# A fused retention and feed-forward kernel: another order of loads, products and vector work in its first block

## The chip, the core and the metric

The kernel runs on one core of a Trainium2 chip. The metric is the device time of one execution in microseconds, where less is better. Besides the times of whole executions there is one profiled execution, whose trace gives the start and the length of every instruction on the engines: PE (TensorE, with PEld for its weight loads), DVE (VectorE), ACT (ScalarE), POOL (GpSimd) and SP (SyncE, which here only issues DMAs).

## The reference

Per batch and head a state is carried along the sequence, and the result goes through a feed-forward layer. Inputs are float32, with 4 batches, 8 heads, 768 positions and a head dimension of 64; the layer has 512 inputs and 2048 hidden units.

```python
gamma = 1.0 - 2.0 ** (-5.0 - np.arange(H))
for t in range(S):
    state = gamma * state + np.einsum('bhd,bhe->bhde', k[:, :, t], v[:, :, t])
    y[:, :, t] = D ** -0.5 * np.einsum('bhd,bhde->bhe', q[:, :, t], state)
x = y.transpose(0, 2, 1, 3).reshape(B * S, H * D)      # 3072 x 512
h = x @ w_in                                           # 512 x 2048
g = h * np.tanh(np.log1p(np.exp(h)))                   # Mish
out = g @ w_out                                        # 2048 x 512
```

## The kernel before

The 3072 tokens are 24 chunks of 128 tokens. A chunk's attention is done in matrix form: the scores of its keys against its queries (`scores`), a triangular mask with the decay folded into q and v (`mask`, on DVE), the product of the masked scores with v (`present`), the product of q with the state of the chunks before (`past`), and the update of the state by an outer product of k and v (`outer`). Present and past add up in one bank of PSUM, and a copy on ACT turns the sum into `xt`, the input of the layer. The layer is done by blocks of chunks: the first block has four chunks (512 tokens, `CPB` = 4), and the ten blocks that follow have two each. All inputs are cast to float16 on the way, with sums in float32.

The layer's matrix products save multiplications by the scheme of seven products in place of eight (Strassen's, in Winograd's form). For that, sums of quarters of each operand are made on DVE: `wsums` from w_in, `tmats` from w_out (`weight_sums`, four for each half), `gsums` from g, and `tsums` from x. In the first block the first product (`g1`) is done plainly, with 16 steps of 128 hidden units each followed by a Mish on ACT. Its second product (`first_g2`) takes the seven products for the slices 0 and 2 of w_out, each slice having 512 hidden units, and plain products for the slices 1 and 3; the plain products of slice 3 (`end`) close each output. Each product in `first_g2` is done for two pairs of chunks, and the results meet in four banks: `px`, `pz`, `pb` and `pe`.

The order of instructions on each engine is the order in which the code emits them, because the schedule is manual: every engine has its own queue and works through it in order, and semaphores make it wait for its operands and for buffers. Work that another engine's progress should delay is put in at a named point: `plan` in `first_block` lists what is emitted after which step of the first product, and `late` is a list of small DVE jobs that `some_late(n)` takes from the front. `gate(x)` is a tiny copy on POOL that makes all POOL work behind it wait until x is written.

Buffers come from pools that rotate. The staging pool `rn_wstage` has four buffers of 8 KB per partition under the tag `wt`: they hold in turn the first block's q, the four slices of w_in, output slices, and then the float16 sums. Another pool, with the tag `g`, has two buffers that hold the other two output slices and later g. PSUM has four banks for products (`mm`) and two double banks for attention (`at`), each reused in rotation: a tile waits until the one before it in the same place has been read.

In the first block the queries come in two halves by heads (`load_first_q`, line 200), and k and v come for two pairs of chunks (s = 0 and 1) and two halves of heads each (`load_two`). `turn_first_q` and `turn_two` transpose on PE, `first_q_out` and `turned_two` copy the result out of PSUM, `cast_two` casts k on ACT and v on POOL. `spin` and `spin_wide` are matmuls whose results are not used. From line 802 on, `first_block` writes out the order: casts and turns, `scores_half` and `mask_half` for the four combinations of s and half, `outer_first` and `state_first` for the states, `present_first` and `past_first` for the output of attention, `xt_out`, and then the first product, of which the first two steps are split into halves of tokens (`first_g1`). `load_weights` (line 778) issues the loads of the weights on SP's queue, and behind them q and v of the chunks 4 and 5 (`load_one`); `load_more` issues the last output slice in two halves and q and v of the next chunks. k of the later chunks is brought by POOL's own DMA queue (`bring_k`). `first_g2` also holds the attention of the chunks 4 and 5, which the second block takes as its input (`y_two(1, False)` near its end).

Of the kernel before, what the change touches and what calls it, by code (L numbers as in the profile page):

```python
# [16 lines left out]
def kernel(  # L17
# [135 lines left out]
    def load_w(which, s):  # L153
        if which == "in":
            t = wstage.tile([P, NBP, TB], FP32, name="wi", tag="wt", bufs=4)
            n = TB // 2 if s < 2 else TB
            for o in range(0, TB, n):
                nc.sync.dma_start(t[:, :, o:o + n], win_ap[:, :, s * TB + o:s * TB + o + n])
        else:
            if s < NSL // 2:  # L160
                t = wstage.tile([P, FPS, d_model], FP32, name="wt", tag="wt", bufs=4)
            else:
                t = gp.tile([P, FPS, d_model], FP32, name="wt", tag="g")
            if s < NSL - 1:
                nc.sync.dma_start(t, wout_ap[:, s * FPS:(s + 1) * FPS])  # L165
        wtmps[which, s] = t
# [31 lines left out]

    def load_first_q():

        qf = wstage.tile([P, H, CPB, D], FP32, name="qfirst", tag="wt", bufs=4)
        for a in range(0, H, H // 2):
            nc.sync.dma_start(
                qf[:, a:a + H // 2],
                q[0, a:a + H // 2, :TB].rearrange("h (p r) d -> p h r d", r=CPB))
        return qf

    def turn_first_q(qf, half):
        a, n = half * (H // 2), H // 2
        q16 = castp.tile([P, CPB, n, D], FP16, name="qfirst16", bufs=1, tag=f"qfirst16_{half}")  # L210
        nc.vector.tensor_tensor(
            q16.rearrange("p r h d -> p h r d"), qf[:, a:a + n],
            qs_spread[:, a:a + n].unsqueeze(3).broadcast_to((P, n, CPB, D)), op=ALU.mult)
# [6 lines left out]
    def first_q_out(half, t_ps, eng):  # L220
        n = HP // 2
        dst = qfirst_t[:, half * n:(half + 1) * n].rearrange("p i (t r) -> p i t r", r=CPB)
        src = t_ps.rearrange("p i r t -> p i t r")
        if eng is nc.scalar:
            nc.scalar.copy(dst, src)
        else:
            eng.tensor_copy(dst, src)

# [29 lines left out]

    def turned_two(s, half):
        n = HP // 2  # L260
        nc.scalar.copy(kts[s][:, half * n:(half + 1) * n], t16s.pop((s, half)))

# [58 lines left out]

    def xt_out(g, y, eng, n=1):
        if eng is nc.scalar:
            nc.scalar.copy(xts[0][:, g:g + n], y[:, g % 2:g % 2 + n])
        else:
            eng.tensor_copy(xts[0][:, g:g + n], y[:, g % 2:g % 2 + n])

# [450 lines left out]
    def load_weights():  # L778
        for s in range(NSL):
            load_w("in", s)  # L780
        for s in range(NSL):
            load_w("out", s)
        room(CPB)
        room(CPB + 1)
        for g in (CPB, CPB + 1):
            load_one(g, 0, nc.sync)
            load_one(g, 2, nc.sync)

    def load_more():
        load_last_wout(0)  # L790
        load_last_wout(1)
        nload[0] += 2
        load_to(CPB + 4)
# [7 lines left out]

    def first_block():
        qf = load_first_q()
        for s in range(2):
            for nm in "kv":
                for half in range(2):
                    load_two(nm, s, half)
        nload[0] = CPB
# [6 lines left out]
        spin(at, 8)  # L815
        tq = turn_first_q(qf, 0)
        spin_wide(at, 3)
        first_q_out(0, tq, nc.scalar)
        tq = [tq, turn_first_q(qf, 1)]
# [21 lines left out]
        state_first(0)  # L841
        at = at_tile()
        scores_half(1, 0, at)
        mask_half(1, 0, at)
        y = atps.tile([P, 2, HP, C], FP32, name="y_ps", tag="at")
        present_first(0, y, range(HP))
        turn_two(1, 1)
        turned_two(1, 1)
        state_first(1)
        past_first(1, y)  # L850
        xt_out(0, y, nc.scalar, 2)
        for half in range(2):
            cast_two("v", 1, half)
        cast_win(0, 0, nc.gpsimd)
        at = at_tile()
        scores_half(1, 1, at)
        mask_half(1, 1, at)
        y = atps.tile([P, 2, HP, C], FP32, name="y_ps", tag="at")
        outer_first(1)
        state_first(2)  # L860
        present_first(1, y, range(HP // 2))
        h_ps = [mmps.tile([P, 1, TB], FP32, name="h_ps", tag="mm") for _ in range(2)]
        first_g1(h_ps[0], 0, 0)
        present_first(1, y, range(HP // 2, HP))
        past_first(2, y)
        past_first(3, y)
        xt_out(2, y, nc.scalar)
        xt_out(3, y, nc.vector)
        first_g1(h_ps[1], 1, 0)
# [5 lines left out]
        for s in range(1, NSL):  # L875
            for half in range(2):
                cast_win(s, half, nc.vector)
            if s == 2:
                late.extend(win_sums())
            if s >= 2:  # L880
                some_late(4)
        room_for_sums()
        plan = {9: [(cast_wout, 0), (room_for_more,), (bring_first,)],
                10: [(some_late, 1)], 13: [(cast_wout, 1), (room_for_more,)], 16: [(load_more,)]}
        late.extend(weight_sums(0) + weight_sums(1))
        for u in range(2, NFB):
            g1(0, u)
            for fn, *args in plan.get(u + 1, ()):
                fn(*args)
        first_g2()  # L890
        hsnaps.append(gp.tile([P, 4, TB], FP32, name="hsnap", tag="g0"))

    def bring_first():
        gate(wtmps["out", 1][:, 0, :1])
        bring_k(CPB)
        bring_k(CPB + 1)

    def first_g2():
        hf = d_model // 2
        sub = ALU.subtract  # L900
        pairs = range(CPB // 2)
# [25 lines left out]

        def g_part(s, i):
            g = gtiles[0, s // 2][:, s % 2 * FPS:(s % 2 + 1) * FPS]
            return g.rearrange("p f (a i t) -> p f a i t", a=2, i=2)[:, :, :, i]  # L930

        def g_sum(dst, x, y, f):
            d = sums[:, dst - 1].rearrange("p f (a t) -> p f a t", a=2)
            nc.vector.tensor_tensor(d, x, y, op=f)

        def the_sum(i):
            return sums[:, i - 1].rearrange("p f (a t) -> p f a t", a=2)
# [4 lines left out]
        g_sum(1, g_part(0, 1), g_part(2, 1), ALU.add)  # L942
        g_sum(2, the_sum(1), g_part(0, 0), sub)
# [8 lines left out]
        some_late(1)  # L952
        g_sum(3, g_part(0, 0), g_part(0, 1), sub)
        g_sum(4, g_part(2, 0), the_sum(2), sub)
        some_late(1)
        for p in pairs:
            mm(pz[p], a(p, 1, 1), b(1, 1))
        for p in pairs:
            mm(pb[p], a(p, 0, 1), b(1, 0))
        for p in pairs:  # L960
            mm(pb[p], a(p, 0, 2), b(2, 0))
        for p in pairs:
            mm(pe[p], a(p, 0, 1), b(1, 1))
        for p in pairs:
            mm(px[p], sm(p, 2), t(2))
            nc.scalar.copy(osb[p][0][:, 1], px[p])
        turn(CPB, True)
        for p in pairs:
            mm(px[p], sm(p, 3), t(3))
            nc.vector.tensor_tensor(osb[p][1][:, 1], px[p], m5[p], op=ALU.add)  # L970
        bring_k(CPB + 2)
        cast_v(CPB + 1)
        bring_k(CPB + 3)
        for p in pairs:
            mm(pe[p], sm(p, 4), b(2, 1))
        some_late(1)
        scores(CPB)
        turn(CPB + 1)
        mask(CPB)
        cast_wout(3, FPS)  # L980
        for p in pairs:
            mm(px[p], a(p, 1, 2), t(4))
# [18 lines left out]

        end(0, 0)
        end(0, 1)
        y_two(1, False)
# [102 lines left out]
```

## Time and profile before

| | |
|---|---|
| Time, median of 3 executions | 200.63 us (200.55 to 201.08) |
| The profiled execution | 200.17 us |
| Its span, from the first to the last instruction | 198.4 us |
| PE busy in the span | 190.2 us (96%) |
| DVE busy | 144.8 us (73%) |
| ACT busy | 114.9 us (58%) |
| POOL busy | 82.5 us (42%) |
| Granted TensorE clock | 1.0 all along |
| Moved by DMA | 36.05 MB, 182 GB/s on average |

A line of the order in time gives the start and the length of a group of like instructions in microseconds, the engine, the line of the kernel, the operation, what it writes and reads, the shape, and how many there are; in brackets stands how long the engine was idle before it and what ended that. A line of the busy times by stretch gives the stretch, its length, the busy time and number of instructions of each engine in it, the granted clock, the share of time in which the DMA engines were busy, and what they moved in GB/s. A busy engine is the bound of a stretch only where nothing makes it wait; where PE has gaps, what ended them has to be looked for.

### The profile page before, as it was taken

What the parts mean: (1) busy time and instruction counts of PE and PEld (TensorE: products, weight loads), DVE (VectorE), ACT (ScalarE), POOL (GpSimd) and SP (SyncE); (2) the same over time, 40 slices, a digit from 0 to 9 for tenths busy, and PEclk for the clock granted to TensorE, in tenths of its full rate; (3) what the DMA queues carried; (4) which work ended last, traced back from release to release, by engine and by line L of the source; (5) the groups of instructions that cost most, each with busy time, mean ns of one, the idle gap of its engine ahead of it and who ended that gap; (6) DMA issues with size and microseconds to landing.
All of it is one profiled execution on the core that took longest, in us unless ns stands there. A gap on an engine that the chain in (4) does not pass through costs nothing.

```text
span 198.4 us, 5725 instructions
## 1 busy us (share of the span) xinstructions
PE 190.2 (96%) x2363; PEld 157.7 (79%) x2363; DVE 144.8 (73%) x294; ACT 114.9 (58%) x220; POOL 82.5 (42%) x110
## 2 busy tenths in 40 slices
PE   6897999999999999999999999999999999999992
PEld 2355546974987988988988988988988988988982
DVE  3786698998898597597498597597498596596362
ACT  2463667243673675675664774774754765765840
POOL 7072005695646708708606707707615614110000
PEclk9999999999999999999999999999999999999999
DMA  5999999999999999997997996997996967201102
GB/s 170 302 311 354 384 388 318 196 298 176 166 259 225 180 188 226 202 145 156 188 162 156 157 168 146 179 176 93 244 195 84 202 90 61 102 3 53 56 26 79
DMA packets 95897, 36.05 MB, mean 182 GB/s; under 512 B 82304, under 2 KB 89984, under 8 KB 95872
## 3 DMA queue, kind: packets, MB, share of 16 engines
q1 hardware_dynamic: 74928, 33.04, 76.3%
q0 software_dynamic: 20800, 2.62, 21.0%
q8 instruction: 18, 0.29, 0.7%
q14 instruction: 7, 0.06, 0.1%
q10 hardware_dynamic: 144, 0.03, 0.1%
HBM read 27.30 MB, written 6.29 MB: 169 GB/s over the span
## 4 chain that ended last, share of the span: by engine, by line
PE 78%; SPq 7%; DMA 6%; DVE 4%; ACT 2%; issue 1%; DVEq 0%
PE o_ps L727 30%; PE h_ps L654 18%; PE h_ps L630 16%; SPq L140 5%; DMA wt<-in_moe_w_out_dram 4%; PE y_ps L463 3%; PE at L397 3%; DMA qfirst<-in_q_dram 2%; PE y_ps L454 2%; PE o_ps L924 2%; PE h_ps L798 1%; SPq L165 1%; PE u_ps L412 1%; DVE gsum L705 1%; SPq L170 1%
## 5 line engine op out<-in xcount | busy, mean ns | idle before, releaser
L654 PE MATMUL h_ps<-xt,win 128*128 128x256 f16 x320 | 41.5, 273 | 0.0
L647 DVE TENSOR_TENSOR hsum<-h_ps,hsnap 128x512 f32<-128x512 f32 x30 | 19.8, 688 | 20.9 <-PE h_ps L630 18.9
L727 PEld LDWEIGHTS <-gsum 128*128 128x128 f16 x320 | 30.8, 98 | 4.0 <-DVE gsum L705 0.4
L654 PEld LDWEIGHTS <-win 128*128 128x128 f16 x320 | 29.3, 98 | 3.6
L727 PE MATMUL o_ps<-tmat,gsum 128*128 128x256 f16 x240 | 27.8, 273 | 0.0
L727 PEld LDWEIGHTS <-g 128*128 128x128 f16 x240 | 23.3, 98 | 2.9
L641 ACT ACTIVATE g<-hsum 128x512 f16<-128x512 f32 x30 | 18.6, 630 | 11.4 <-DVE hsum L647 11.2
L403 DVE TENSOR_TENSOR am<-at,tri 128x1024 f16<-128x1024 f32 x20 | 24.3, 1215 | 0.0
L347 POOL TENSOR_TENSOR v<-vf,qvs 128x512 f16<-128x512 f32 x20 | 23.5, 1177 | 0.4 <-PE o_ps L924 0.4
L661 ACT ACTIVATE g<-h_ps 128x512 f16<-128x512 f32 x40 | 22.9, 603 | 0.8 <-PE h_ps L654 0.6
L637 ACT COPY hsnap<-h_ps 128x512 f32<-128x512 f32 x30 | 16.4, 582 | 11.2 <-PE h_ps L630 11.2
L336 POOL TENSOR_TENSOR qk<-qf,qvs 128x512 f16<-128x512 f32 x20 | 21.6, 1080 | 2.1 <-DMA qf<-in_q_dram 2.1
L355 POOL COPY gate<-gsum 128x1 f16<-128x1 f16 x9 | 1.6, 183 | 48.4 <-DVE gsum L701 48.4
L741 DVE TENSOR_TENSOR osb<-o_ps,snap 128x256 f32<-128x256 f32 x30 | 12.5, 418 | 12.4 <-PE o_ps L727 10.9
L733 ACT COPY snap<-o_ps 128x256 f32<-128x256 f32 x30 | 11.2, 372 | 16.0 <-PE o_ps L727 15.7
L630 PEld LDWEIGHTS <-wsum 128*128 128x128 f16 x320 | 19.5, 98 | 0.5
L727 PE MATMUL o_ps<-wout,g 128*128 128x256 f16 x160 | 19.3, 273 | 0.0
L342 POOL DMA_DIRECT2D qk<-in_k_dram x20 | 18.8, 942 | 0.0
L630 PE MATMUL h_ps<-xsum,wsum 128*128 128x128 f16 x240 | 16.7, 219 | 0.0
L500 ACT CAST xt<-y_ps 128x1024 f16<-128x1024 f32 x10 | 10.1, 1013 | 10.6 <-PE y_ps L454 10.6
L630 PEld LDWEIGHTS <-win 128*128 128x128 f16 x240 | 15.1, 98 | 0.7
L435 ACT COPY stx<-stc 64x256 f16<-64x256 f16 x30 | 12.0, 400 | 2.0 <-POOL stc L429 1.8
(119 smaller groups left out, 306.9 us busy)
## 6 DMA issues: line engine op xcount, KB each, us to landing
vf<-in_v_dram SPq DMA_DIRECT2D x24, 256.0 KB, 5.7
out_dram<-osb SPq DMA_DIRECT2D x22, 256.0 KB, 4.9
qf<-in_q_dram SPq DMA_DIRECT2D x20, 256.0 KB, 5.4
wt<-in_moe_w_out_dram SPq DMA_DIRECT2D x3, 1024.0 KB, 8.9
qk<-in_k_dram POOLq DMA_DIRECT2D x20, 128.0 KB, 5.5
wi<-in_moe_w_in_dram SPq DMA_DIRECT2D x4, 512.0 KB, 7.3
wi<-in_moe_w_in_dram SPq DMA_DIRECT2D x2, 1024.0 KB, 11.3
qfirst<-in_q_dram SPq DMA_DIRECT2D x2, 512.0 KB, 5.1
```

The source lines that it names most:

```text
L336: nc.gpsimd.tensor_tensor(room16(g)[0], loaded[g][0], qs.unsqueeze(2).broadcast_to((P, H, D)), op=ALU.mult)
L342: nc.gpsimd.dma_start(room16(g)[1], k[b, :, c * C:(c + 1) * C].rearrange("h p d -> p h d"))
L347: nc.gpsimd.tensor_tensor(room16(g)[2], loaded[g][2], vs.unsqueeze(2).broadcast_to((P, H, D)), op=ALU.mult)
L403: nc.vector.tensor_tensor(am, ats.pop(g), tri.unsqueeze(1).unsqueeze(1).broadcast_to((P, 2, HP, C)), op=ALU.mult)
L630: nc.tensor.matmul(h_ps[:, f], w(f, d), x(d), start=first and f == 0 and d == 0, stop=d == n - 1, skip_group_check=True)
L637: nc.scalar.copy(x, h_ps)
L641: nc.scalar.activation(gt[:, 2 * i * FPS:(2 * i + 1) * FPS, j * P:(j + 1) * P], h, AF.Mish, scale=inv_boost3)
L647: nc.vector.tensor_tensor(h, h_ps, x, op=ALU.add)
L654: nc.tensor.matmul(h_ps[:, j], win(s, 2 * half + j, bp), xt(blk, bp), start=bp == 0, stop=bp == NBP - 1)
L661: nc.scalar.activation(gt[:, fb:fb + 2], h_ps, AF.Mish, scale=inv_boost3)
L727: nc.tensor.matmul(o_ps, x(f), w(f), start=first and f == 0, stop=f == n - 1, skip_group_check=True)
L741: nc.vector.tensor_tensor(dst, o_ps, plus, op=ALU.add)
```

## The change

It reorders the first block; the computation is the same.

- Front: k's first half of heads is loaded before the second half of q. The cast of q is taken out of its transposition. The second half of q is cast half on DVE and half on POOL, after the turn of k's first part, and turned only after the first scores and mask. Copies change engines: the second half of q goes out on ACT instead of DVE, the turned k of s = 0 on DVE instead of ACT; `xt_out` is one ACT copy of two chunks each time. One of the unused products goes. `outer_first(0)` stands ahead of the turn of the next k; y of the first two chunks comes after the last scores and mask instead of before; the casts of the second v come earlier.
- Output slices: they are loaded in the order 0, 2, 1, 3; slices 0 and 2 lie in the staging pool, 1 and 3 in the other. The two halves of slice 3 are issued among q and v of the chunks 4 and 5 instead of after them. Slices 1 and 3 are cast half on DVE and half on ACT.
- First product: four of the eight sums of w_in are left for later (`wsum_late`). The sums of g are made during the first product (`g_sum`) instead of in `first_g2`, with the casts of slices 0 and 2 and the first four sums of w_out between them.
- Second product: the products of slices 0 and 2 come first, the plain ones of slice 1 after them. POOL's gate ahead of the casts of chunk 4 is on the last of the four sums of w_out instead of the second. At the end, one sum of w_out, the scores and the mask of chunk 5 and the outer product of chunk 4 come behind `end(0, 0)` instead of ahead of it, with the outer product behind the scores and the mask.

The core of the diff:

```diff
-            if s < NSL // 2:
+            if s % 2 == 0:
                 t = wstage.tile([P, FPS, d_model], FP32, name="wt", tag="wt", bufs=4)
...
+    def cast_first_q(half, engines):
...
+        m = n // len(engines)
+        for e, eng in enumerate(engines):
+            b = slice(a + e * m, a + e * m + m)
+            eng.tensor_tensor(
+                q16[:, :, e * m:e * m + m].rearrange("p r h d -> p h r d"), raw["q"][:, b],
+                qs_spread[:, b].unsqueeze(3).broadcast_to((P, m, CPB, D)), op=ALU.mult)
...
-    def turned_two(s, half):
+    def turned_two(s, half, on_act=False):
...
+        if on_act:
+            nc.scalar.copy(dst, src)
+        else:
+            nc.vector.tensor_copy(dst, src)
...
+    def xt_out(g, y):
+        nc.scalar.copy(xts[0][:, g:g + 2], y)
...
-        for s in range(NSL):
+        for s in (0, 2, 1, 3):
             load_w("out", s)
...
+        load_one(CPB, 0, nc.sync)
+        load_one(CPB, 2, nc.sync)
+        load_last_wout(0)
+        load_one(CPB + 1, 0, nc.sync)
+        load_last_wout(1)
+        load_one(CPB + 1, 2, nc.sync)
...
     def first_block():
...
+        load_first_q(0)
+        load_two("k", 0, 0)
+        load_first_q(H // 2)
+        load_two("k", 0, 1)
...
+        cast_first_q(0, [nc.vector])
+        tq = turn_first_q(0)
         cast_two("k", 0, 0)
         turn_two(0, 0)
-        first_q_out(1, tq[1], nc.vector)
+        first_q_out(0, tq)
         turned_two(0, 0)
-        cast_two("k", 0, 1)
         spin_wide(at, 3)
+        cast_first_q(1, [nc.vector, nc.gpsimd])
         scores_half(0, 0, at)
         mask_half(0, 0, at)
+        cast_two("k", 0, 1)
+        tq = turn_first_q(1)
+        first_q_out(1, tq)
...
         cast_two("k", 1, 0)
+        outer_first(0)
         turn_two(1, 0)
-        turned_two(1, 0)
+        turned_two(1, 0, True)
         cast_two("k", 1, 1)
-        outer_first(0)
         state_first(0)
+        for half in range(2):
+            cast_two("v", 1, half)
...
             if s == 2:
                 late.extend(win_sums())
-            if s >= 2:
                 some_late(4)
         room_for_sums()
-        plan = {9: [(cast_wout, 0), (room_for_more,), (bring_first,)],
-                10: [(some_late, 1)], 13: [(cast_wout, 1), (room_for_more,)], 16: [(load_more,)]}
         late.extend(weight_sums(0) + weight_sums(1))
+        wsum_late = [late.pop(0) for _ in range(4)]
+        plan = {9: [(g_sum, 3)],
+                12: [(g_sum, 1), (cast_wout, 0), (room_for_more,), (bring_first,), (g_sum, 2),
+                     (some_late, 1)],
+                14: [(cast_wout, 2), (room_for_more,), (some_late, 2), (g_sum, 4),
+                     (some_late, 1)],
+                16: [(load_more,)]}
...
         for p in pairs:
             mm(pe[p], sm(p, 1), t(1), True)
             nc.scalar.copy(m5[p], pe[p])
-        cast_wout(2)
-        some_late(1)
-        gate(tmats[0][:, 1, 0, :1])
+        for p in pairs:
+            mm(pb[p], a(p, 0, 2), b(2, 0))
+        for p in pairs:
+            mm(px[p], sm(p, 2), t(2))
+            nc.scalar.copy(osb[p][0][:, 1], px[p])
+        cast_wout(1, 2)
+        gate(tmats[1][:, 1, 0, :1])
         casts(CPB)
         cast_q(CPB + 1)
...
+        for p in pairs:
+            mm(px[p], sm(p, 3), t(3))
+            nc.vector.tensor_tensor(osb[p][1][:, 1], px[p], m5[p], op=ALU.add)
+        for p in pairs:
+            mm(pe[p], sm(p, 4), b(2, 1))
+        for fn in wsum_late:
+            fn()
+        for p in pairs:
+            mm(px[p], a(p, 1, 2), t(4))
         for p in pairs:
             mm(pb[p], a(p, 0, 1), b(1, 0))
         for p in pairs:
+            mm(pz[p], a(p, 1, 1), b(1, 1))
         turn(CPB, True)
         bring_k(CPB + 2)
         cast_v(CPB + 1)
         bring_k(CPB + 3)
         for p in pairs:
+            mm(pe[p], a(p, 0, 1), b(1, 1))
         scores(CPB)
+        cast_wout(3, 2)
+        mask(CPB)
         turn(CPB + 1)
         for p in pairs:
             mm(px[p], a(p, 1, 1), b(1, 0))
-        outer_wide(CPB)
         casts(CPB + 2)
         turn_and_load(CPB + 2)
         cast_q(CPB + 3)
-        scores_one(CPB + 1)
-        decay_wide(CPB)
...
         end(0, 0)
+        some_late(1)
+        scores_one(CPB + 1)
+        outer_wide(CPB)
+        decay_wide(CPB)
         end(0, 1)
         y_two(1, False)
```

More of the change, by code (lines that the diff above doesn't have):

```diff
@@ L218, in turn_first_q, with first_q_out @@
         return t_ps
-    def first_q_out(half, t_ps, eng):
+    def first_q_out(half, t_ps):
         n = HP // 2
[L222 to L227, printed above, removed]
+        nc.scalar.copy(
+            qfirst_t[:, half * n:(half + 1) * n].rearrange("p i (t r) -> p i t r", r=CPB),
+            t_ps.rearrange("p i r t -> p i t r"))
     def load_two(nm, s, half):
@@ L320, in past_first @@
                 start=False, stop=True, skip_group_check=True)
[L322 to L326, printed above, removed]
+    def xt_out(g, y):
+        nc.scalar.copy(xts[0][:, g:g + 2], y)
     def room16(g):
@@ L836, in first_block @@
         cast_two("k", 1, 0)
+        outer_first(0)
         turn_two(1, 0)
-        turned_two(1, 0)
+        turned_two(1, 0, True)
         cast_two("k", 1, 1)
-        outer_first(0)
         state_first(0)
+        for half in range(2):
+            cast_two("v", 1, half)
         at = at_tile()
@@ L844, in first_block @@
         mask_half(1, 0, at)
-        y = atps.tile([P, 2, HP, C], FP32, name="y_ps", tag="at")
-        present_first(0, y, range(HP))
+        state_first(1)
         turn_two(1, 1)
[L848 to L854, printed above, removed]
+        turned_two(1, 1, True)
         at = at_tile()
@@ L889, in first_block, with g_sum, part, first_g2 @@
                 fn(*args)
-        first_g2()
+        first_g2(wsum_late)
         hsnaps.append(gp.tile([P, 4, TB], FP32, name="hsnap", tag="g0"))
     def bring_first():
-        gate(wtmps["out", 1][:, 0, :1])
+        gate(wtmps["out", 2][:, 0, :1])
         bring_k(CPB)
         bring_k(CPB + 1)
-    def first_g2():
+    def g_sum(n):
+        def part(s, i):
+            g = gtiles[0, s // 2][:, s % 2 * FPS:(s % 2 + 1) * FPS]
+            return g.rearrange("p f (a i t) -> p f a i t", a=2, i=2)[:, :, :, i]
+        s1, s2, s3, s4 = [
+            gsums[0].rearrange("p s (f a) t -> p s f a t", a=2)[:, i] for i in range(4)]
+        dst, x, y, f = {
+            1: (s1, part(0, 1), part(2, 1), ALU.add), 2: (s2, s1, part(0, 0), ALU.subtract),
+            3: (s3, part(0, 0), part(0, 1), ALU.subtract),
+            4: (s4, part(2, 0), s2, ALU.subtract)}[n]
+        nc.vector.tensor_tensor(dst, x, y, op=f)
+    def first_g2(wsum_late):
         hf = d_model // 2
-        sub = ALU.subtract
         pairs = range(CPB // 2)
```

80 lines of the change are left out of this document (19 added, 61 removed).

## The prediction

> **What bounds the kernel now.** I read the page's first part for the bound, then busy time by stretch for where that bound breaks down, then the order of time in the first block, where all of the edits lie.
>
> ```profile
> PE 190.2 (96%) x2363; PEld 157.7 (79%) x2363; DVE 144.8 (73%) x294; ACT 114.9 (58%) x220; POOL 82.5 (42%) x110
> ```
>
> ```profile
> 0.00:20.70 20.70, 16.45 (x235) 9.41 (x236) 12.98 (x30) 8.86 (x14) 8.85 (x19) 1.00 1.00 288
> 20.70:32.80 12.10, 12.10 (x58) 5.49 (x57) 10.25 (x18) 8.40 (x15) 1.05 (x1) 1.00 1.05 383
> 32.80:49.78 16.98, 16.76 (x173) 12.58 (x172) 15.19 (x20) 7.12 (x12) 12.88 (x13) 1.00 1.43 223
> 49.78:195.00 145.22, 144.88 (x1901) 130.21 (x1899) 106.02 (x227) 90.50 (x180) 59.70 (x79) 1.00 0.94 147
> ```
>
> The columns after the length are the busy times of PE, PEld, DVE, ACT and POOL, the granted clock, the DMA share and GB/s. From 49.78 us, where the second block starts, PE is busy 144.88 of 145.22 us. Nothing can be regained there, so I take a shift of that start to reach the end one for one. Only the first block has to be worked out: the attention front (to 20.7), the first product (to 32.8), and the output product with the next chunks' attention (to 49.78, DVE busy 15.19 of 16.98).
>
> The front and the tail of the first block, in order of time:
>
> ```profile
> 9.68 2.08 POOL L245 TENSOR_TENSOR v<-vf,qvs 128x512 f16<-128x512 f32 x2 [5.17 <-DMA vf<-in_v_dram]
> ...
> 10.01 0.42 PE L274 MATMUL at<-qfirst_t,qkt 64*64 64x128 f16 x16
> ...
> 18.87 0.69 DVE L326 CAST xt<-y_ps 128x512 f16<-128x512 f32 x1 [1.50 <-ACT xt L324]
> 19.30 1.36 PE L798 MATMUL h_ps<-xt,win 128*128 128x256 f16 x11 [0.97 <-issue]
> ```
>
> ```profile
> 37.28 1.50 POOL L336 TENSOR_TENSOR qk<-qf,qvs 128x512 f16<-128x512 f32 x1
> ...
> 37.79 1.53 DVE L934 TENSOR_TENSOR gsum<-g,gsum 128x1024 f16<-128x1024 f16 x1
> ...
> 42.39 0.69 DVE L388 COPY qkt<-t_ps 128x1024 f16<-128x1024 f16 x1 [0.17 <-PE t_ps L383]
> ...
> 42.99 1.22 DVE L403 TENSOR_TENSOR am<-at,tri 128x1024 f16<-128x1024 f32 x1
> ...
> 44.20 1.04 ACT L186 CAST wout<-wt 128x1024 f16<-128x1024 f32 x1 [0.43 <-DMA wt<-in_moe_w_out_dram]
> ...
> 44.36 0.69 DVE L445 TENSOR_TENSOR su<-u_ps,st 128x512 f32<-128x512 f32 x1
> ...
> 44.96 1.21 DVE L403 TENSOR_TENSOR am<-at,tri 128x1024 f16<-128x1024 f32 x1
> 45.29 0.96 PEld L924 LDWEIGHTS <-g 128*128 128x128 f16 x5 [0.37 <-issue]
> 46.09 0.92 DVE L449 TENSOR_TENSOR st<-su,gcm 128x512 f16<-128x512 f32 x1
> 46.67 0.48 PEld L463 LDWEIGHTS <-v 128*64 128x64 f16 x16 [0.42 <-issue]
> ...
> 48.84 0.69 DVE L995 TENSOR_TENSOR osb<-o_ps,osb 128x512 f32<-128x512 f32 x1 [0.89 <-PE o_ps L924]
> ```
>
> The reader is to see two things. The last half of output slice 3 lands at 44.17, its ACT cast ends at 45.25, and PE loses 0.37 for it. And the Vector work between the next two chunks' scores and PE's use of the new state (mask, su, mask, st: 42.99 to 47.0) ends just as PE comes to the second "past" product at about 47.3, so it is hidden with nothing to spare.
>
> **The front.** The first k half (256 KB) goes ahead of the second q half. Eight pieces between q's landing at 6.83 and v's last give some 0.92 us each (v at 9.68 is the third, at 13.22 the seventh). So k lands at about 6.2 and the last half of q at 7.75 instead of 6.83; its cast, now half on DVE (0.62) and half on POOL (1.06 by L245), ends at 8.9, and POOL has nothing else until v at 9.68. The ACT cast of k (0.62) moves under DVE's q cast, DVE takes the 0.4 of the copy out (half of L388's 0.69), and the first scores start after ACT's q copy at 8.4, not 10.01. That 1.6 us does not carry. The bytes ahead of v are the same, so POOL's first two v casts still end at 11.8. The outer products now stand ahead of the next turn on PE's queue, so turn and scores of the second half follow them: turn 12.3, ACT copy to 13.3 (0.59), scores 13.3, mask 13.9 to 15.1 (now 13.81 to 15.02), state to 15.8 (0.69), last mask to 17.0, last state to 17.7. PE then does four products of y (0.42), the early h (0.55) and the past (0.45) to 18.4; one ACT copy of both chunks (1.02 by L324) replaces 0.59 on ACT followed by 0.69 on DVE, and ends at 19.6, where the old pair ended at 19.56. Eight matmuls later the first product runs on at 20.6 (now 20.71). Worth -0.1, with -0.5 to +0.4 as bounds, the lower if the masks leave DVE earlier, the upper from a repeat of part of the 0.97 "issue" gap. The warming product that goes (0.86) filled idle time. The second pair of v casts moves earlier in POOL's order but waits for its landing (13.22) as now.
>
> **The loads.** Slices are 1 MB each; the casts that waited show landings at 31.70 and 34.51, so 2.8 apart. In the order 0, 2, 1, 3 slice 2 takes slice 1's place and the other way round; slice 0 may be issued earlier, because its buffer is released by a DVE cast that no longer stands behind an xt copy, but the queue is full (383 GB/s) and I give nothing for it. On SP's queue the halves of slice 3 pass q and v of chunk 5. A 256 KB q or v takes some 1.3 there (estimate: two halves of slice 3 landed 1.5 apart, four such loads lie between slice 2 and the first half, 8.2 us with k's), so slice 3 is complete at about 42.6 and q of 5 lands at 41.1 instead of before 40.2, v of 5 near 44. Cast time of slice 3 stays 1.05 on ACT, now beside 0.69 on DVE. The wait of 0.37 goes; what is late next is Vector work.
>
> **The Vector line up to the seven products.** Four sums of w_in (4 x 0.42) leave 27.7 to 29.2 for later, one g sum (0.68) goes in, and then the second (with slice 2 of g) waits for the Mish of the twelfth product, about 30.05 (the sixteenth ends at 33.6, one per 0.865). So DVE idles some 1.6. From there: sum 0.68, slice 0 cast 1.22 (32.0), sum 0.69, weight sum 0.69 (33.4), slice 2 cast 1.22 (34.65), two weight sums (36.05), sum 0.69, weight sum 0.69 (37.45), half of slice 1 0.69, two additions 0.74 (38.9). The single-time 0.69 instead of 1.53 is right as POOL's gate now waits for the fourth weight sum. PE, at 0.87 per product (32.80 to 33.67): first 32.7, second 33.6, third would start at 34.45 and waits for slice 2, +0.25; the fourth and fifth use the same bank without a turn between them, so the fifth waits for ACT's copy (it starts 0.63 after the fourth starts, then 2 x 0.4), +0.2; the seventh waits for the additions, +0.2; then two plain products, the turn of chunk 4 at 41.2, one product, and scores, which need ACT's qkt copy: 1.7 after the turn starts (38.91 to 40.57 now, with two products between), so +0.35 at 42.9. POOL's casts of 4 and q of 5 end by 42.2, in time for the turn of 5 at 43.2. Total on this stretch +1.0, of which 0.13 was already there before the scores; bounds 0 and +1.6.
>
> **The tail.** From scores at 42.9: scores 0.3, turn 0.45, product 0.87, end(0,0) starts 44.5. Its DVE addition comes 1.14 after that start (47.70 to 48.84): 45.65 to 46.3. Behind it on DVE's queue stand, in program order, a late weight sum, the mask of chunk 5, su and st; now the mask is done at 46.2 and waits for no end product. The weight sum is 0.69 alone (L550) and up to 1.53 beside POOL (L553); POOL then casts chunk 6, so 1.2. Mask 1.21 (48.7), su 0.69, st 0.68 to 0.92: 50.2. PE has only scores, outer, end(0,1) and at most three quarters of y (0.3 + 0.33 + 0.87 + 0.8) for it; y's bank is that of the mask's scores, so y starts at 48.7 and its last part at 50.25. Then 0.25, end 0.87, outer 0.25, end 0.87: the second block starts at 52.4, not 49.78.
>
> **The sum.** 52.4 - 49.78 = +2.6, already holding -0.1 from the front and the 0.37 that slice 3 gives back. The profiled execution took 200.17 (span 198.4, 1.8 around it), so 202.8 for it; it lies 0.46 below the median of the three runs, 200.63, and against that I say 203.2.
>
> [...] The row first: two pairs of POOL casts and DVE f16 sums that overlap took 1.5 each, against 1.04 and 0.69 apart. [...]
>
> **The rivals.**
> (1) The tail is dearer and partly hidden: scores at the earliest 41.9, every DVE row at its bare time. From scores 1.6 to end(0,0), 1.14, then 0.69 + 0.69 + 1.21 + 0.69 + 0.69, then 2.24: 50.85, +1.1, 201.7. For it: each wait on the middle stretch is under 0.4. Against: it needs none of them.
> (2) Faster: the place is end(0,0). If state and mask of chunk 5 are ready when PE reaches y, only the earlier slice 3 (-0.37) and the shorter wait ahead of the scores (-0.2) remain: 200.63 - 0.6 = 200.0. The point from which it decides: DVE would have to finish addition, sum, mask, su and st (4.0 by rows) within the 2.0 or so that PE's work covers behind the addition's start. Nothing in the rows says that; it is so only if DVE does not keep this order.
> (3) POOL's casts hold up DVE at the four w_in sums (1.7 alone, three POOL operations of 1.04 between them) and in full at the late sum and st (0.84 and 0.24 more): mask of chunk 4 at 43.7 instead of 43.4, then +0.7: +3.6, 204.2. For it: the 1.53 rows. Against: POOL waits for q of 5 meanwhile.
> (4) No change: gains and waits cancel within 0.3% (0.6 us, about what a measurement here can tell); that takes a tail of +0.6, less than any sum above.
>
> **How the numbers follow.** The forecast (+2.0 to +3.1) 0.55; rival 1 0.15, rival 2 0.10, rival 3 0.15, rival 4 0.05. The predicted time is 203.2; 201.3 reaches below rival 1 and 204.4 above rival 3, leaving rivals 2 and 4 and a little outside. Faster 0.10, same 0.05, slower 0.85.
>
> **What would show it.** In the changed profile: first scores near 8.4 but the steady first product near 20.6; the g sum of slice 2 at 30; no DMA wait ahead of end(0,0); PE idle of over 1 us between end(0,1) and y, ended by DVE's mask, and a shorter one ended by st; the second block near 52.4, PE without gaps afterwards. I am wrong if the mask of chunk 5 runs before end(0,0)'s addition, if the first product starts more than 1 us earlier, or if PE is not saturated behind the second block's start.

## The result, and the profile after

The changed kernel takes 207.17 us (median of 4 executions, 206.66 to 207.71), the kernel before 200.86 us beside it (200.55 to 201.16). The ratio is 1.0326, with a 95% interval of 1.0304 to 1.0348: it is 6.3 us slower. The forecast was slower as well, but by 2.6 us, and 207.17 lies above the range. Of all the executions behind this document one stands apart and is left out of its ratio: 206.54 us, with a mean granted clock of 0.99, among seven of the kernel before with the loads of the change. The profiled execution of the changed kernel took 206.66 us, with a span of 204.9 us.

The page's first part, its row of the granted clock, and the busy times by stretch (the same columns as before):

```profile
PE 190.7 (93%) x2361; PEld 158.5 (77%) x2361; DVE 147.0 (72%) x295; ACT 115.3 (56%) x219; POOL 82.3 (40%) x111
...
PEclk9999999998899999999999999999999999999999
```

```profile
20.70:33.00 12.30, 12.30 (x60) 5.77 (x59) 9.64 (x17) 8.41 (x15) 1.20 (x2) 1.00 1.05 380
33.00:57.00 24.00, 20.65 (x208) 15.50 (x207) 19.17 (x30) 8.01 (x15) 12.42 (x14) 0.93 1.26 217
57.00:200.00 143.00, 141.11 (x1855) 126.75 (x1853) 104.87 (x219) 89.19 (x178) 58.75 (x77) 1.00 0.85 138
```

PE does the same work, 190.7 us against 190.2. The first product still runs without a gap. What is new is 3.35 us of idle PE between 33 and 57 us, a clock below 1.0 in that stretch, and 1.9 us of idle PE behind 57 us, where the kernel before had 0.34 in the whole rest.

The tail of the first block, in order of time, all engines:

```profile
45.07 0.94 POOL L343 DMA_DIRECT2D qk<-in_k_dram  x1
...
45.35 0.69 DVE L994 TENSOR_TENSOR osb<-o_ps,osb 128x512 f32<-128x512 f32 x1 [0.53 <-PE o_ps L943]
...
45.95 2.68 DVE L551 TENSOR_TENSOR tmat<-wout 128x1024 f16<-128x1024 f16 x1
46.03 1.06 POOL L337 TENSOR_TENSOR qk<-qf,qvs 128x512 f16<-128x512 f32 x1
...
47.03 1.04 POOL L348 TENSOR_TENSOR v<-vf,qvs 128x512 f16<-128x512 f32 x1
...
48.56 1.21 DVE L404 TENSOR_TENSOR am<-at,tri 128x1024 f16<-128x1024 f32 x1
...
49.83 1.07 PE L464 MATMUL y_ps<-am,v 128*64 128x128 f16 x16 [3.06 <-DVE am L404]
...
50.40 0.69 DVE L450 TENSOR_TENSOR st<-su,gcm 128x512 f16<-128x512 f32 x1
```

The addition of end(0,0), the late weight sum (L551), the mask of chunk 5 and the state (`st`) stand behind one another on DVE, as forecast; between mask and state comes `su`, the old state plus the outer product. But the sum takes 2.68 us, where such a sum alone takes 0.68: it starts 0.06 us before the end of a DMA issue on POOL (45.07 to 46.01, the instruction with which POOL starts a load of k) and ends 0.56 us after the second of the two POOL casts that follow the issue without a gap. PE waits 3.06 us for the mask, where the kernel before had no wait. Then the clock falls. Busy times by stretch around that place:

```profile
48.00:50.00 2.00, 0.17 (x5) 0.17 (x6) 2.00 (x3) 0.00 (x0) 1.12 (x2) 0.93 1.13 111
50.00:51.00 1.00, 1.00 (x18) 0.83 (x16) 0.96 (x2) 0.00 (x0) 0.00 (x0) 0.50 1.05 188
...
52.00:53.00 1.00, 1.00 (x4) 0.30 (x2) 0.00 (x0) 0.91 (x1) 0.00 (x0) 0.50 1.25 278
53.00:54.00 1.00, 1.00 (x12) 0.41 (x11) 0.55 (x1) 0.00 (x0) 0.00 (x0) 0.93 1.39 214
```

The clock is at 0.50 for some 3.4 us (from 49.7 to 53.1, worked out from the mean clocks of the stretches). end(1,0), nearly all of it in that time, takes from 51.65 to 53.35, 1.70 us where it took 0.96. The second block starts at 54.47 instead of 49.78. In it stands a second stall, again in order of time:

```profile
57.27 0.94 POOL L343 DMA_DIRECT2D qk<-in_k_dram  x1
...
57.80 3.04 DVE L553 TENSOR_TENSOR tmat<-wout,wout 128x1024 f16<-128x1024 f16 x1
...
58.23 1.06 POOL L337 TENSOR_TENSOR qk<-qf,qvs 128x512 f16<-128x512 f32 x1
...
59.24 1.04 POOL L348 TENSOR_TENSOR v<-vf,qvs 128x512 f16<-128x512 f32 x1
...
60.76 1.27 DVE L648 TENSOR_TENSOR hsum<-h_ps,hsnap 128x512 f32<-128x512 f32 x2
...
61.50 0.61 PE L631 MATMUL h_ps<-xsum,win 128*128 128x128 f16 x8 [1.57 <-DVE hsum L648]
```

The same weight sum in the kernel before, with the same DMA issue, but a pause of POOL between the issue and the cast:

```profile
52.59 0.94 POOL L342 DMA_DIRECT2D qk<-in_k_dram  x1
...
53.12 0.68 DVE L552 TENSOR_TENSOR tmat<-wout,wout 128x1024 f16<-128x1024 f16 x1
...
53.85 1.03 POOL L336 TENSOR_TENSOR qk<-qf,qvs 128x512 f16<-128x512 f32 x1 [0.33 <-DMA qf<-in_q_dram]
```

In both kernels the sum starts 0.53 us into the issue. With the pause it takes 0.68. Without it, it takes 3.04 and again ends 0.56 after POOL's second cast; the addition behind it is late, and PE waits 1.57 us. So the shift of the profiled span, 204.9 - 198.4 = 6.5 us, is 4.7 at the second block's start, 1.6 in its stall and 0.2 elsewhere.

### The profile page after: what moved, and what is told of

Same layout as the page of the kernel before. It is cut to its first block, busy times and chain, and to the rows that moved or that the text cites. A ratio compares the mean times of both kernels' runs of the same rounds, so it can differ in the third digit from the quotient of the medians.

```text
span 204.9 us, 5720 instructions
## 1 busy us (share of the span) xinstructions
PE 190.7 (93%) x2361; PEld 158.5 (77%) x2361; DVE 147.0 (72%) x295; ACT 115.3 (56%) x219; POOL 82.3 (40%) x111
## 4 chain that ended last, share of the span: by engine, by line
PE 85%; DVE 8%; DMA 2%; issue 2%; ACT 2%; DVEq 0%
PE o_ps L728 29%; PE h_ps L655 16%; PE h_ps L631 14%; PE o_ps L943 6%; PE h_ps L516 6%; PE y_ps L464 3%; PE at L398 3%; PE y_ps L455 2%; DMA qfirst<-in_q_dram 2%; DVE qfirst L211 1%; DVE tmat L551 1%; DVE am L404 1%; PE h_ps L800 1%; PE u_ps L413 1%; DVE gsum L706 1%
## 5 line engine op out<-in xcount | busy, mean ns | idle before, releaser
L337 POOL TENSOR_TENSOR qk<-qf,qvs 128x512 f16<-128x512 f32 x20 | 20.7, 1036 | 2.1 <-DMA qf<-in_q_dram 2.1
L343 POOL DMA_DIRECT2D qk<-in_k_dram x20 | 19.5, 973 | 0.0
```

What stands on the lines that cost most here:

```text
L337: nc.gpsimd.tensor_tensor(room16(g)[0], loaded[g][0], qs.unsqueeze(2).broadcast_to((P, H, D)), op=ALU.mult)
L343: nc.gpsimd.dma_start(room16(g)[1], k[b, :, c * C:(c + 1) * C].rearrange("h p d -> p h d"))
```

## The experiments

Two theories were put against each other. Theory A: DVE's queue in the tail is the cause, with sums that wait for POOL's casts. Theory B: the earlier parts of the change (front, loads, slice order, products) set the time, and the tail only shows it. In the kernels that follow, all of the computation is done. Times are medians; each ratio is to the kernel before on the same chip. The kernel before took 200.74 to 200.88 us beside the various runs, so differences between runs of different groups are good to some 0.1 us. What is said of single instructions is read from one profiled execution of each kernel.

**One part undone: the attention ahead of end(0,0) again.**

```diff
+        outer_wide(CPB)
         casts(CPB + 2)
         turn_and_load(CPB + 2)
         cast_q(CPB + 3)
+        scores_one(CPB + 1)
+        decay_wide(CPB)
...
         end(0, 0)
         some_late(1)
-        scores_one(CPB + 1)
-        outer_wide(CPB)
-        decay_wide(CPB)
         end(0, 1)
```

> The changed kernel with one part undone: the outer product of chunk 4, the scores and mask of chunk 5 and the decay stand ahead of end(0,0) again, as in the kernel before; the late weight sum stays behind end(0,0). Theory A (DVE's queue in the tail): the mask of chunk 5 waits for neither the addition of end(0,0) nor the late sum, y starts near 46.8 instead of 49.8, PE has no gap over 0.7 us there, the clock stays 1.0, the second block starts near 50.2 instead of 54.5, and the time is 202.8 if the second stall (PE 1.6 us at 61.5) stays, 201.0 if it goes with it. Theory B (the order of loads and casts earlier in the block sets the time, the tail only shows it): over 205.

Measured: 203.88 us, from 201.35 to 204.13 in ten executions, ratio 1.0127 (1.0094 to 1.0159). Theory B's bound of 205 is not reached by any of them. In the profiled execution, the fastest (201.35), y starts at 47.03 without a wait, the clock is 1.0 and the second block starts at 50.30; its weight sum took 2.05 and PE lost 0.42 there. There POOL paused 0.49 for a load behind the first cast, and the sum waited for that one cast only. So the order of the tail is worth over 3 us, but something still moves the time by 2.8 us from execution to execution.

**Only the late sum moved behind the state.**

```diff
         end(0, 0)
-        some_late(1)
         scores_one(CPB + 1)
         outer_wide(CPB)
         decay_wide(CPB)
+        some_late(1)
         end(0, 1)
```

> The changed kernel with the late weight sum alone moved behind the decay of the state, everything else as it is. Theory A: mask at 46.05, su 47.3, st 48.0 to 48.7, y at 47.3 and its last part at 48.7, gap on PE some 0.6 us, clock 1.0, second block near 50.9: 203.6 with the second stall, 201.9 without it. If the order of mask, su and st behind the addition were the whole loss and the sum's 2.7 us were hidden: 206 or more. Theory B: over 205.

Measured: 203.34 us, ratio 1.0135 (1.0117 to 1.0153), 0.3 from the first of the two forecasts. The mask ran at 45.93, y began at 47.20 after a gap of 0.46, the clock stayed at 1.0 in the tail. The second stall stays: its sum took 2.96, and PE waited 1.02 there. PE also waited 0.36 for the state, and 0.62 ahead of the second block for ACT's xt copy. On ACT's queue that copy stands behind the copy of end(0,1), which waits for DVE's addition, and the late sum, again at 1.53, stood ahead of that addition.

**POOL held back, DVE's order as it is.**

```diff
-        casts(CPB + 2)
-        turn_and_load(CPB + 2)
-        cast_q(CPB + 3)
...
         end(0, 0)
         some_late(1)
+        gate(tmats[0][:, 0, FPS, :1])
+        casts(CPB + 2)
+        turn_and_load(CPB + 2)
+        cast_q(CPB + 3)
         scores_one(CPB + 1)
```

> The changed kernel with DVE's order as it is, but POOL's casts of chunk 6 and of q of chunk 7 held back by the gate copy until the late weight sum is written. If the sum took 2.7 us because it waited for POOL's casts: it takes 0.69 now (or 0.9), mask near 46.8, y near 48.0, PE's gap 1.2 instead of 3.1, clock 1.0, second block near 51.6, time 204.3 with the second stall and 202.5 without it. If the 2.7 us is the instruction's own time at that place (its operands, its buffer): unchanged, 207.

Measured: 204.32 us (204.30 to 204.34), ratio 1.0181 (1.0165 to 1.0196), as forecast. The order of time on DVE in this kernel:

```profile
45.60 0.69 DVE L991 TENSOR_TENSOR osb<-o_ps,osb 128x512 f32<-128x512 f32 x1 [0.53 <-PE o_ps L943]
46.20 0.68 DVE L551 TENSOR_TENSOR tmat<-wout 128x1024 f16<-128x1024 f16 x1
46.80 1.22 DVE L404 TENSOR_TENSOR am<-at,tri 128x1024 f16<-128x1024 f32 x1
```

The same instruction at the same place takes 0.68 when POOL is idle. Its 2.68 was a wait for POOL, and with the clock that it brought down it cost 2.85 us by the medians.

**Unused products in PE's gap.**

```diff
         end(0, 1)
+        for _ in range(12):
+            nc.tensor.matmul(
+                t0[0].rearrange("p a (b t) -> p (a b) t", t=P), ident,
+                ident.unsqueeze(1).broadcast_to((P, HP, P)), start=True, stop=True)
         y_two(1, False)
```

> The changed kernel with twelve unused 512-column products on PE in the gap ahead of y (into a bank that has been read). If the granted clock of 0.5 between 50 and 53.3 us comes from the 3.06 us of idle PE and costs time: the clock stays 1.0, end(1,0) takes 1.0 instead of 1.76, the second block starts some 1.2 us earlier, 206.0. If the low clock costs nothing because PE waits for the state anyway: 207.2, the same.

Measured: 205.38 us (204.59 to 206.15), ratio 1.0233 (1.0200 to 1.0266). The granted clock stays at 1.0, and end(1,0) goes from 51.87 to 52.83, 0.96 us. The drop of the clock in the changed kernel thus comes from the emptiness of PE: 3.06 us in one piece there, waits of 0.71 and 0.36 here. By the medians it costs some 1.8 us, which is close to half of the 3.4 us at 0.50; the four executions spread over 1.6 us. In the profiled one, the slowest of the four, the late sum took 2.92.

**The kernel before with the tail alone.**

```diff
-        some_late(1)
         scores(CPB)
...
-        outer_wide(CPB)
         casts(CPB + 2)
         turn_and_load(CPB + 2)
         cast_q(CPB + 3)
-        scores_one(CPB + 1)
-        decay_wide(CPB)
...
         end(0, 0)
+        some_late(1)
+        scores_one(CPB + 1)
+        outer_wide(CPB)
+        decay_wide(CPB)
         end(0, 1)
```

> The kernel before with the tail of the change alone: late weight sum, scores and mask of chunk 5, outer product and decay of chunk 4 behind end(0,0), in the order of the change; loads, front and the order of products as before. Theory A (the tail's order, with a late sum that waits for POOL): end(0,0)'s addition near 46, late sum 0.7 to 2.7, y not before 48.5, second block between 52.3 and 54.5 instead of 49.8: 203.2 to 205.5, the more if the second stall comes with it. Theory B (the tail is dear only with the new loads and products): within 0.5 of 200.7.

Measured: 205.22 us, ratio 1.0242 (1.0202 to 1.0281): 4.5 of the 6.3 us, without any of the other parts. PE's longest waits behind the attention front, in the profiled execution (206.74, the slowest of four):

```profile
PE h_ps L630 <- DVE hsum L647: 1.6, 1, 1.6
PE y_ps L463 <- DVE am L403: 1.1, 1, 1.1
PE y_ps L454 <- DVE st L449: 1.0, 1, 1.0
...
PE o_ps L924 <- ACT wout L186: 0.7, 1, 0.7
```

Here the late sum took 0.68, since POOL's next cast waited for its load, and the forecast's waits are all there: for the mask 1.1, for the state 1.0. The second stall came too. In this execution the clock fell to 0.50 near 50.9, although no wait in the tail was longer than 1.1; its mean was 0.991. In the other three executions, which took 205.09 to 205.23, the mean was 0.997 to 0.999, too high for such a drop, so the 4.5 us do not contain it. Theory B falls with this run as the main cause.

**The kernel before with the front alone.**

```diff
-        qf = load_first_q()
-        for s in range(2):
-            for nm in "kv":
...
+        load_first_q(0)
+        load_two("k", 0, 0)
+        load_first_q(H // 2)
+        load_two("k", 0, 1)
...
+    def xt_out(g, y):
+        nc.scalar.copy(xts[0][:, g:g + 2], y)
```

The casts, copies and order of the front up to the first product are those of the change; sums, slices and products are as before.

> The kernel before with the front of the change alone: k ahead of the last half of q, casts and copies on other engines, order of scores, masks, states and y, one unused product less. Theory A: the gain of the first scores (10.0 to 7.9) does not carry, the steady first product starts at 20.5 to 20.7 and the time is 200.7 within 0.4. Theory B: the front costs or gains more than 0.6.

Measured: 200.72 us, ratio 1.0004 (0.9993 to 1.0015). The front is worth nothing, as forecast: the steady first product starts at 20.51.

**POOL held back at both places.**

The edit of the run that held POOL back, and in the second block:

```diff
-            "p7": [(cast_q, a), (some_late, 1), (sums_a, blk, slice(0, FPS))],
+            "p7": [(gate, tmats[1][:, 0, FPS, :1]), (cast_q, a), (some_late, 1),
+                   (sums_a, blk, slice(0, FPS))],
```

> The changed kernel with POOL held back at both places: the casts of chunk 6 until the late weight sum is written (as in the run that held POOL back), and in the second block the cast of q behind a gate on the third of the remaining weight sums. If the second stall (PE 1.57 us until 61.5) is the weight sum that waits for POOL's casts standing one behind the other: that sum takes 0.7 to 1.2 instead of 3.04, PE does not wait there, and the time is 202.8, which leaves the order of the tail as forecast. If the stall has another cause (too much Vector work for the stretch): 204.3 as without it.

Measured: 202.82 us (202.69 to 203.04), ratio 1.0102 (1.0080 to 1.0124), as forecast. The sum of the second block, which the gate keeps POOL away from:

```profile
55.74 0.68 DVE L553 TENSOR_TENSOR tmat<-wout,wout 128x1024 f16<-128x1024 f16 x1
```

The second stall is gone and gives back 1.5 us. What is left over the kernel before is 2.1 us, and PE waits 1.1 for the mask and 0.8 for the state: this is the order of the tail that the prediction worked out. The clock stayed at 1.0 through these two waits in the profiled execution.

**The tail of before and the gate in the second block.** The edit of the first run together with the gate of the last one.

> The changed kernel with the tail of before and the gate in the second block. The run with the tail of before alone took 201.35 to 204.13, and in the profiled one, the fastest, the weight sum of the second block waited 2.05. If that sum is what spreads the times: steady at 200.9 to 201.3, no more than 0.6 above the kernel before, with loads, front, and products as in the change. If the spread comes from elsewhere: still 201.4 to 204.

Measured: 202.01 us (200.95 to 202.36), ratio 1.0057 (1.0041 to 1.0074): 0.7 above the first forecast and inside the second. The stall of the second block is gone, but the product of su with the decay (the state) met POOL's two casts of chunk 6, which stood without a gap, and took 1.93 instead of 0.68; its end, 48.36, lies 0.55 after theirs. PE waited 0.45 for it, and 0.95 for the xt copy, which came late over ACT's queue in the same way as above. A spread of 1.4 us is left of the first run's 2.8, so the sum of the second block was part of it, and this place is probably another.

**The kernel before with the loads of the change.**

```diff
-        for g in (CPB, CPB + 1):
-            load_one(g, 0, nc.sync)
-            load_one(g, 2, nc.sync)
+        load_one(CPB, 0, nc.sync)
+        load_one(CPB, 2, nc.sync)
+        load_last_wout(0)
+        load_one(CPB + 1, 0, nc.sync)
+        load_last_wout(1)
+        load_one(CPB + 1, 2, nc.sync)
```

(the two calls of `load_last_wout` go from `load_more`; the order of the slices stays 0, 1, 2, 3)

> The kernel before with one part of the loads of the change: the halves of output slice 3 are issued among q and v of chunk 5. Slice 3 is there before end(0,0) and PE's 0.37 wait goes, but q of chunk 5 lands near 41.2 instead of before 40.2, so its cast and the turn of chunk 5 (41.7) come later by 0.6 or more: 200.9 within 0.5 if the second block stays as it is. If the later loads of chunk 5 push POOL's casts together so that weight sums wait for them as in the changed kernel, 202 and more.

Measured: 201.83 us, ratio 1.0053 (1.0032 to 1.0074). That lies between the two forecasts. In the profiled execution, the slowest of the six compared (202.84, the others 201.75 to 201.94), PE's 0.37 for slice 3 is gone, but the turn of chunk 5 waits 0.60, and v of chunk 5 is cast at 44.65 instead of 42.58. POOL's casts, pushed together, then find their loads landed. In order of time in the second block:

```profile
54.00 3.04 DVE L552 TENSOR_TENSOR tmat<-wout,wout 128x1024 f16<-128x1024 f16 x1
```

The order of the loads alone brings the second stall, 1.57 us of PE in this execution, into the kernel before.

**Slice 3 ahead of v of chunk 5 only.**

```diff
+        load_one(CPB, 0, nc.sync)
+        load_one(CPB, 2, nc.sync)
+        load_one(CPB + 1, 0, nc.sync)
+        load_last_wout(0)
+        load_last_wout(1)
+        load_one(CPB + 1, 2, nc.sync)
```

> The kernel before with the halves of output slice 3 ahead of v of chunk 5 only (q of chunk 5 keeps its place). The wait of 0.37 goes, v of chunk 5 lands near 44 and is needed at 47: 200.3. If POOL's later casts fall on the mask, su and st of the tail: 200.8 to 202.

Measured: 201.59 us, ratio 1.0029 (1.0015 to 1.0043), so the second, dearer forecast. The state took 1.86 beside POOL's cast of q of chunk 6, and the second block's sum 2.05; PE lost 0.62 and 0.58.

**No critical sum beside a cast.** The changed kernel with the tail of before, the gate in the second block, the late sum behind y, and POOL's casts of chunk 6 behind the new state:

```diff
+        outer_wide(CPB)
+        scores_one(CPB + 1)
+        decay_wide(CPB)
+        gate(states[CPB][:, 0, :1])
         casts(CPB + 2)
...
         y_two(1, False)
+        some_late(1)
```

> The changed kernel with its front, loads, slice order and products, but the tail of before, the late weight sum behind y, POOL's casts of chunk 6 behind the new state, and the gate in the second block: no Vector sum of the critical line lies beside a POOL cast. Theory A: second block near 50.2, no stall in it, 200.9 to 201.3, and the spread of the earlier runs with the tail of before (201.35 to 204.13, 200.95 to 202.36) is gone. If loads, slice order and products cost more by themselves: 202 or more.

Measured: 201.90 us (201.65 to 202.16), ratio 1.0047 (1.0031 to 1.0064). The spread is gone, the time is 0.6 above the forecast. PE's waits in order of time:

```profile
50.44 0.32 PE L413 MATMUL u_ps<-v,qk 128*64 128x64 f16 x8 [0.88 <-POOL v L348]
```

POOL held back is now itself late: the outer products of chunk 6 need its v cast, and PE waits 0.88 for it. That accounts for nearly all of the 1.0 us over the kernel before; loads, slice order and products leave little else. The order of the slices and that of the products were not run by themselves.

**A version to beat both.** The kernel before with slice 3 ahead of v of chunk 5, the DMA of k of chunk 7 ahead of that v's cast on POOL, and the gate in the second block:

```diff
         bring_k(CPB + 2)
+        bring_k(CPB + 3)
         cast_v(CPB + 1)
-        bring_k(CPB + 3)
```

> The kernel before with the halves of output slice 3 ahead of v of chunk 5, the DMA of k of chunk 7 ahead of that chunk's v cast on POOL (so POOL fills its wait and the casts behind it start 0.9 earlier), and the gate in the second block that keeps POOL's q cast behind the weight sums. In the run with the loads alone PE lost 0.62 to the state, which waited 1.2 for POOL's cast of q of chunk 6, and 0.58 to the second block's weight sum, and gained the 0.37 of slice 3. If these two waits are the whole loss: 200.4, 0.2% under the kernel before. If the state still meets that cast: 200.9 or more.

Measured: 200.74 us, ratio 1.0000 (0.9987 to 1.0014): no gain, between the two forecasts. The state still met the cast (1.17), and PE waited 0.32 for POOL's v cast of chunk 6. No version here beats the kernel before.

## Why the prediction was right in its direction and wrong in its size

**The front** was right: the steady product starts at 20.50 in the changed kernel (20.6 was worked out), and the front by itself measures 1.0004. The first scores came at 7.87 instead of 10.01, and the 1.6 to 2.1 us do not carry.

**The loads** came as worked out: slice 3's second half was cast from 43.0 (42.6), q of chunk 5 landed at 41.25 (41.1), v of chunk 5 at 44.08 (near 44). That the 0.37 goes was right. What was missed is their after-effect. The prediction named late v of chunk 5 but gave it no price; it pushes POOL's casts together, and that is the main way in which these loads cost 1.0 us even in the kernel before.

**The Vector line up to the seven products** was right within 0.4: the g sum of slice 2 at 29.96 (30.05) after 1.51 of idle DVE, scores of chunk 4 at 42.55 (42.9), the addition of end(0,0) at 45.35 (45.65).

**The tail** was right in order and place: with the sums freed from POOL the changed kernel costs 2.1 us over the kernel before, against the 2.6 forecast; with 0.69 for the sum instead of 1.2 the forecast would have been 2.1 too. The term that failed is the late weight sum, put at 1.2 between 0.69 and 1.53. It measured 2.68, outside both ends. The upper end was taken from sums that had started while a cast ran and had waited for that one (37.79 to 39.32, beside a cast from 37.28 to 38.78). The late sum started during the DMA issue directly ahead of two casts without a gap, and it waited for both. The third rival had this mechanism and named the place, but at 0.84 more for the sum it priced one cast as well, and 204.2 was too low.

**The granted clock** was no term at all. The forecast left PE a gap of over 1 us without asking what the clock does. Behind the gap that came, of 3.06 us, it fell to 0.50 for some 3.4 us, which costs some 1.8 by the run that fills the gap; the run that holds POOL back gives back 2.85 for clock and sum together.

**The step "PE is saturated behind the second block's start, so a shift reaches the end one for one"** failed. The kernel before has no wait there over 0.25, but only because POOL's cast of q waited 0.33 for its load at 53.5, which let the weight sum run in 0.68. With the casts in one run the sum took 3.04 and PE lost 1.57; the gate on it gives back 1.5. The prediction named this as a thing that would make it wrong, and gave it no chance in the range.

Taken away one after the other: 207.17 as changed, 204.32 with POOL held back at the late sum, 202.82 with POOL held back at the second sum too. The last is within 0.5 of the 203.2 that was forecast for what it did count.

## What to carry to other kernels

A duration taken from a trace holds for the neighbours that the instruction had there: for a Vector sum that reads SBUF alone and may fall beside POOL work, look where in POOL's order it will start. In these traces a sum that started while a cast ran nearly always waited for that cast only (1.53 at 37.79 in the kernel before, where the one ahead of it took 0.69), and one that started late in a DMA issue with casts directly behind it waited for all of them that stood without a gap (2.68 and 3.04 in the changed kernel). A shift is passed on one for one only if the engines that are off the bound keep their pauses; a load that comes earlier or later can close a pause that some other engine lived on, as POOL's 0.33 at 53.5 here. And when a forecast opens a gap on PE, ask what the granted clock does after it: here it was 0.50 for some 3.4 us behind a gap of 3.06.

## What the runs showed of the hardware that was not expected

- A VectorE sum with both inputs in SBUF waited for two POOL casts in a row. The late sum ended 0.56 after the second cast (48.63 and 48.07), the second block's sum 0.56 after it (60.84 and 60.28), and the state in the run with the tail of before and the gate 0.55 (48.36 and 47.81); alone each takes 0.68. Masks, whose scores come from PSUM, kept 1.21 to 1.23 beside casts (1.21 at 48.56 in the changed kernel, beside the cast of 48.75 to 49.79).
- Such a sum did not always wait for the whole run of casts. In five of the changed kernel's later blocks it got its turn between two casts without a gap, and the second cast was the one that was drawn out, to 1.49 us in place of 1.03. The first of them:

```profile
81.99 1.03 POOL L337 TENSOR_TENSOR qk<-qf,qvs 128x512 f16<-128x512 f32 x1
...
82.52 1.05 DVE L706 TENSOR_TENSOR gsum<-g,gsum 128x1024 f16<-128x1024 f16 x1
82.99 1.49 POOL L348 TENSOR_TENSOR v<-vf,qvs 128x512 f16<-128x512 f32 x1
```

The sums that waited for two casts started during the DMA issue directly ahead of them, with one exception: the state at 46.43, which started 0.67 into the first cast. Where POOL paused 0.33 or more behind the issue, the sum ran in 0.68 (the kernel before at 53.12, the gated kernel at 55.74). Why a sum that starts late in the issue is held up already then, and loses its turn between the casts, no run here settles.

- The clock fell to 0.50 after 3.06 us of idle PE and came back near 53.1. In the profiled execution of the kernel before with the tail alone it fell as well, near 50.9, with no wait over 1.1 us in the tail. In the 4 us in which it came down PE was busy 0.94 us (46 to 50) and 1.93 us (47 to 51). In the run that held POOL back the emptiest 4 us (46 to 50, and 47 to 51) have PE busy 2.17 us, and the clock did not fall in its profiled execution; yet its emptiest 3 us, 47 to 50, have 1.17, less than the 1.32 of 48 to 51, where the second drop came. So that drop came without a single long gap, with waits of 1.1 and 1.0 us and work between them. What share of work keeps the clock up, and over what time, is left open.
